# Pacing the bulk transfers of a fused attention and MLP kernel by the exponentials

## The chip, the cores and the metric

One core of a Trainium2 chip runs the whole kernel. The metric is the device time of one execution in microseconds, as the median of several runs. TensorE is written PE (and PEld for its weight loads), VectorE DVE, ScalarE ACT, GpSimd POOL, and SyncE SP; SP hands all transfers to the 16 DMA engines in one queue, in the order in which they stand on it.

## The reference

`x` has 2048 rows of 512 columns; there are 32 heads of 16 columns each, and the hidden layer has 1792 columns.

```python
x = A_x
xn = layernorm(x)                       # mean and variance over the 512 columns, eps 1e-5
qkv = xn @ wqkv                         # 512 x 1536, split into q, k, v of 32 heads x 16
p = softmax(q @ k.T * 16 ** -0.5)       # per head, 2048 x 2048
attn = (p @ v) @ wo
mlp = gelu_tanh(xn @ w1 + b1) @ w2 + b2
out = x + attn + mlp
```

## The kernel before

Precision is kept by pairs: an operand of a dense product is split into a high and a low float16 half, scaled by a power of two, and the product is three float16 products (`PAIRS`). The exponentials and `v` stay float32.

The attention runs over 32 blocks (8 groups of 4 heads, times 4 blocks of 512 queries), and each block over 16 units of 128 keys: 512 units, one after the other. In a unit, `s_half` computes scores for the maxima (`pS` on PE, a maximum on DVE), and `e_half` computes, for the unit that is 20 earlier (`LEAD`), transposed scores (`pT` on PE) and their exponential on ACT (`pe`, four of 128x512 a unit, L343). `v_half` multiplies the exponentials of one or two units before that by `v` (`pV`). Into each unit a planner lays a fixed share of the other dense work (`dense`, bank `pD`). In this text unit n is the one after which the counter `pos` stands at n; block t begins at unit 16t + 1 for the maxima, and at unit 16t + 21 for the exponentials.

In the first part (up to about unit 81) that other dense work is the projection of `q` and `k` for the heads of the later groups. A projection group has three units' worth of products (`project`); ACT copies its result to `pf`, POOL splits it into `stg`, and it is stored in DRAM (`qk_d`). `stacks` loads it from there as `kst` and `qst`, the operands of the scores, some 40 units before they are used. When the maxima of a block are known, DVE transposes them (`mrow`, L312), POOL splits them (`mhl`, L315 to L317), they are stored (`m_d`, L321) and loaded into two rows of each `qst` (L326); the exponentials of the block wait for these rows.

Beside that, the first part prepares the weights of the second (`prepare`): 16 chunks of 512 KB of `w1`, `w2` and `wo` are loaded (`wch`, three buffers), split on POOL in three steps (`split_steps`, to which the code gives costs of 1240, 1240 and 2330 ns; a `stg` pair has 620 and 1160), and the halves of `w1` and `w2` are stored (`wsp`, three buffers, to `w1_d` and `w2_d`, named `w_d` in the profile). Eight of the sixteen pieces of the normalised input are stored in this stage as well (`keep_x`, `xn_d`).

In the second part the other dense work is the MLP: `fetch_w1` loads `wc`, `fetch_x` a block of normalised input `xb` (one buffer, four pieces of 256 KB), and the `w2_s` pieces come one every three units. The third part is the output projection.

The order on every engine is that of the code, which is written unit by unit: `ORDERED` switches any reordering off. After each unit `tick()` runs what is due: `run_due()` calls what `later(n, fn)` has put n slots ahead, and `run_steps()` gives POOL queued steps worth up to `POOL_NS` = 2500 ns a slot. So a transfer stands on SP at the slot at which the code issued it, but SP carries it out as soon as the instructions before it on SP are handed over and what it waits for itself is done; it doesn't wait for the engines to reach that slot.

Of the kernel before, what the change touches and what calls it, by code (L numbers as in the profile page):

```python
# [11 lines left out]
AF = mybir.ActivationFunctionType  # L12
# [14 lines left out]
QB = 512  # L27
# [4 lines left out]
FAST, MEAN, SLOW, LATE = (8, 8), (7, 7), (6, 6), 6  # L32
MEASURE = (3, 0, 1, 2)
HALF = 1300
BEHIND = 4
POOL_NS = 2500
TAIL = 12
# [11 lines left out]
def layer_kernel(ctx: ExitStack, tc: tile.TileContext, x, wqkv, wo, w1, b1, w2, b2, out):  # L49
    nc = tc.nc  # L50
# [187 lines left out]
    def later(n, fn, local=False):  # L238
        queue.append((slot[0] + n, fn, local))

    urgent = []

    def run_due():
        while urgent:
            urgent.pop(0)()
        due = sorted((q for q in queue if q[0] <= slot[0]), key=lambda q: q[0])
        queue[:] = [q for q in queue if q[0] > slot[0]]
        for q in due:
            q[1]()
# [7 lines left out]
    def run_steps(all_of_them=False):  # L257
        room[0] = min(room[0], 0) + POOL_NS
        while steps and (room[0] > 0 or all_of_them):
            ns, fn = steps.pop(0)  # L260
            room[0] -= ns
            fn()

    def tick():
        run_due()
        run_steps()
        slot[0] += 1

    def flush():

        while steps or any(q[2] for q in queue):
            run_due()
            run_steps(True)
            slot[0] += 1

# [56 lines left out]
    def e_half(u, n):  # L332

        p, a = divmod(n, 2)
        t, kt = divmod(u, 16)
        g, qb = divmod(t, NQB)
        st = banks("T")
        r = slice(64 * a, 64 * a + 64)
        k0 = (kt % 4) * P
        tiled(None, st, kst[g % 2][p][kt // 4][r, k0:k0 + P], qst[g % 2][p][qb][r, :], True, True)  # L340
        pe = work.tile([P, QB], F32, name="pe", bufs=12)
        ptiles[u, n] = pe
        nc.scalar.activation(pe, st, AF.Exp, scale=factor(exp_scale, sexp[0:1, g // 2:g // 2 + 1]))  # L343
        given("act", 470)

    def v_half(u, a):
# [90 lines left out]
    def stacks(g, w, blocks):  # L437
        for b in blocks:
            for p in range(2):
                for a in range(2):  # L440
                    h = 4 * g + 2 * p + a
                    nc.sync.dma_start((qst, kst)[w][g % 2][p][b][64 * a:64 * a + 48, :],
                                      qk_d[w, h * DH:(h + 1) * DH, :, b * QB:(b + 1) * QB].rearrange("d j n -> (d j) n"))


# [151 lines left out]
    def fetch_x(b):  # L597
        if b < NQB:
            xbs[b] = feed[0].tile([P, 2, NC, QB], F16, name="xb", bufs=1)
            first = next(d for d in range(1, 17) if b == 0 or 2 <= (pos[0] + d) % 16 <= 11)  # L600
            for c in range(NC):
                later(first + c, lambda c=c: nc.sync.dma_start(xbs[b][:, :, c], xn_d[:, :, c, b * QB:(b + 1) * QB]))

    def fetch_w1(n):
        if n < NQB * NF:
# [107 lines left out]
    with ExitStack() as st1:  # L713
# [10 lines left out]
        def chunk(src):  # L724
            wf = ph.tile([P, 4 * W], F32, name="wch", bufs=3)
            v = wf.rearrange("p (a b) -> p a b", b=src.shape[2])
            if len(loads) < 17:
                nc.sync.dma_start(v, src)
            else:
                later(2, lambda: nc.sync.dma_start(v, src), True)  # L730
            return v

        def absmax(dst, v):
            nc.vector.tensor_reduce(dst, v, axis=AX.XY if len(v.shape) == 3 else AX.X, op=ALU.max,  # L734
# [24 lines left out]
        loads = []  # L759
# [83 lines left out]

        def keep_x(t):
            c, cols = t % NC, slice(t // NC * QB, t // NC * QB + QB)
            nc.sync.dma_start(xn_d[:, :, c, cols], xt[:, :, c, cols])

        def tile_and_unit(t):

# [122 lines left out]
        def prepare():  # L972
            yield from ms
            am = work.tile([P, 10], F32, name="am_all")
            nc.vector.tensor_reduce(am[:, 0:7], amx[:, 0:7, :], axis=AX.X, op=ALU.max)
            nc.vector.tensor_reduce(am[:, 7:8], b1_s, axis=AX.X, op=ALU.max, apply_absolute_value=True)
            nc.vector.tensor_reduce(am[:, 8:9], amx[:, 7:14, :], axis=AX.XY, op=ALU.max)
            nc.vector.tensor_reduce(am[:, 9:10], amx[:, 14:16, :], axis=AX.XY, op=ALU.max)
            box = []
            yield  # L980
            yield from scales(am, 10, sbank, box)
            inv, fac = box
            fac1.append(fac)

            nc.vector.reduce_max(gs[:, 0:1], fac[:, 0:8], axis=AX.X)
            nc.vector.tensor_tensor(gs[:, 3:4], fac_v[0][:, 0:1], fac[:, 9:10], op=ALU.mult)
            yield
            nc.vector.reciprocal(gs[:, 1:2], gs[:, 0:1])
            nc.vector.tensor_tensor(gs[:, 2:3], gs[:, 0:1], fac[:, 8:9], op=ALU.mult)
            yield  # L990
            nc.vector.tensor_scalar_mul(gs[:, 1:2], gs[:, 1:2], 0.5)
            ended = [True]
            for n in range(16):
                v = fetch(16 + n)
                while not ended[0]:
                    yield
                ended[0] = False

                def then(wh=None, n=n):
                    ended[0] = True  # L1000
                    later(2, lambda: put(wh, n), True)

                def put(wh, n):
                    for a in range(2):
                        if n < 7:
                            later(a, lambda a=a: nc.sync.dma_start(w1_d[n, :, a], wh[:, a]), True)
# [18 lines left out]
        ctx.enter_context(tc.manual_schedule(engines=ORDERED))  # L1025
        fil, pre, more = rest(), prepare(), True
        while not spent[0] or more or cur[0] is not None:
            unit(fil)
# [5 lines left out]
    def mlp():  # L1034
# [236 lines left out]
```

## Time and profile before

| | us |
|---|---|
| median of 3 runs (1473.83 to 1477.21) | 1473.98 |
| time of the profiled execution | 1471.34 |
| span of the profiled execution | 1469.5 |
| first exponential | 127 |
| end of the first part, about | 305 |

| queue or engine | |
|---|---|
| bytes moved by SP's transfers | 118.72 MB |
| their packets' time as a share of 16 DMA engines | 26.5% |
| PE, share of the span busy | 98% |
| POOL, share of the span busy | 50% |

A page row of an engine gives its busy time, its share of the span and its instruction count. A stage row gives start, end and length in us, and then for PE, PEld, DVE, ACT and POOL the busy time with the count in brackets, the clock granted to TensorE, the share of time that the DMA engines were busy and the GB/s they moved. A timeline row gives the start, the duration, the engine, the line, the operation, its output and inputs; behind it in square brackets stand the idle time of the engine before it and what ended it. "issue" there is time in which the engine waited for nothing that the profile shows. Chain and wait rows name lines of the code shown above.

### The profile page before, as it was taken

The page shows a single profiled execution, that of the slowest core. Times are in us where ns is not written, and L with a number is a line of the kernel's source. Part 1 is how long each engine was busy: PE and PEld are TensorE (multiplying, and loading weights), DVE is VectorE, ACT ScalarE, POOL GpSimd, SP SyncE. Part 2 cuts the span into 40 slices and gives each one's busy share as a digit, 9 for nine tenths or more (in the row PEclk, how much of TensorE's full clock was granted, in tenths as well). Part 3 has the DMA queues.
Part 4 walks back from the last instruction along what each step waited for, and adds up shares of the span by engine and source line. Part 5 has one row for each costly group of instructions (what it writes and reads, how often), then busy time and mean ns, then how long its engine had stood idle before and what let it go on. Part 6 is the DMA issues. An engine that isn't in the chain of part 4 may idle for free.

```text
span 1469.5 us, 87300 instructions
## 1 busy us (share of the span) xinstructions
PE 1445.6 (98%) x39753; PEld 928.6 (63%) x39753; DVE 1363.0 (93%) x2340; ACT 1230.0 (84%) x2326; POOL 737.5 (50%) x846
## 2 busy tenths in 40 slices
PE   8999989999999999999999999999999999999998
PEld 4434656666666666666666666666666666666674
DVE  7799998999999999999999999999999999999913
ACT  5325877899899999999998999999999999998884
POOL 4113598747766536556553655456475545551100
PEclk9999999999999999999999999999999999999999
DMA  6466457544111211121121211121101211102342
GB/s 205 154 185 176 137 183 241 171 127 117 59 42 44 88 51 37 45 58 53 38 66 45 63 44 45 30 75 50 56 26 54 78 37 35 29 24 73 112 130 102
DMA packets 118023, 124.30 MB, mean 85 GB/s; under 512 B 29080, under 2 KB 89624, under 8 KB 117652
## 3 DMA queue, kind: packets, MB, share of 16 engines
q1 hardware_dynamic: 117652, 118.72, 26.5%
q8 instruction: 310, 5.08, 1.4%
q14 instruction: 61, 0.50, 0.1%
HBM read 80.87 MB, written 37.60 MB: 81 GB/s over the span
## 4 chain that ended last, share of the span: by engine, by line
PE 90%; POOL 4%; DVE 3%; DMA 1%; issue 1%; ACT 1%; SPq 0%; DVEq 0%; POOLq 0%; ACTq 0%
PE pV L195 25%; PE pD L195 23%; PE pT L195 19%; PE pS L291 18%; PE pS L195 2%; PE pT L584 1%; DVE mt L292 1%; PE pV L584 1%; PE pS L485 1%; POOL wsp L969 1%; PE pT L485 1%; DVE amx L734 0%; PE pD L584 0%; PE pD L485 0%; POOL t L1053 0%
## 5 line engine op out<-in xcount | busy, mean ns | idle before, releaser
L292 DVE TENSOR_REDUCE mt<-pS 128x1 f32<-128x512 f32 x2048 | 1270.0, 682 | 35.5 <-PE pS L291 21.6
L343 ACT ACTIVATE pe<-pT 128x512 f32<-128x512 f32 x2048 | 1105.1, 599 | 133.8 <-PE pS L291 64.7
L195 PE MATMUL pV<-pe,vv 64*32 64x512 f32 x8192 | 1088.1, 599 | 0.5 <-issue 0.2
L195 PE MATMUL pT<-qst,kst 64*32 64x512 f16 x8192 | 658.8, 376 | 3.1 <-ACT pe L343 2.1
L291 PE MATMUL pS<-kst,qst 62*32 62x512 f16 x8192 | 621.6, 378 | 6.2 <-DVE mt L292 4.6
L195 PE MATMUL pD<-xb,wc 64*32 64x512 f16 x5376 | 372.0, 374 | 0.0
L195 PE MATMUL pD<-w_s,g 64*32 64x512 f16 (+1 forms) x6144 | 361.4, 348 | 0.6 <-POOL g L1054 0.4
L291 PEld LDWEIGHTS <-qst 62*32 62x32 f16 x8192 | 250.2, 92 | 136.6 <-issue 38.2
L195 PEld LDWEIGHTS <-kst 64*32 64x32 f16 x8192 | 250.3, 93 | 98.3 <-issue 12.7
L195 PEld LDWEIGHTS <-g 64*32 64x32 f16 x6144 | 197.4, 92 | 87.2 <-POOL g L1055 1.1
L195 PEld LDWEIGHTS <-wc 64*32 64x32 f16 x5376 | 178.3, 91 | 98.0
L195 PEld LDWEIGHTS pV<-pe,vv 64*32 64x32 f32 x8192 | 171.0, 105 | 6.6 <-PE pV L195 2.5
L1082 POOL TENSOR_SCALAR hh<-hh,fac,b_s 128x512 f32<-128x512 f32 x56 | 43.0, 768 | 223.9 <-ACT hh L1080 217.8
L195 PE MATMUL pD<-xt,wqk_h 64*32 64x512 f16 x1920 | 128.7, 375 | 2.3 <-issue 1.5
L1109 POOL TENSOR_TENSOR xa<-xa,yt 128x512 f32<-128x512 f32 x32 | 41.1, 1284 | 89.6 <-ACT yt L1107 89.6
L397 POOL TENSOR_TENSOR osb<-osb,rb 128x512 f32<-128x512 f32 x31 | 39.9, 1287 | 89.3 <-DMA rb<-den_d 86.7
L195 PEld LDWEIGHTS <-wqk_h 64*32 64x32 f16 x1920 | 60.8, 92 | 31.0 <-issue 5.9
L1053 POOL TENSOR_TENSOR t<-t,hh 128x512 f32<-128x512 f32 x56 | 71.8, 1282 | 4.7
L1060 POOL TENSOR_TENSOR t<-t,hh 128x512 f32<-128x512 f32 x56 | 71.8, 1281 | 4.7
L1055 POOL TENSOR_TENSOR g<-t,g 128x512 f16<-128x512 f32 x56 | 65.2, 1164 | 4.6
L1146 DVE SCALAR_TENSOR_TENSOR ac<-pS,gs,ac 128x512 f32<-128x512 f32 x20 | 14.4, 743 | 52.0 <-PE pS L195 40.3
L1058 POOL TENSOR_TENSOR t<-hh 128x512 f32<-128x512 f32 x56 | 58.2, 1040 | 4.1
(144 smaller groups left out, 908.1 us busy)
## 6 DMA issues: line engine op xcount, KB each, us to landing
wch<-in_B_w_dram SPq DMA_DIRECT2D x28, 512.0 KB
wc<-w_d SPq DMA_DIRECT2D x56, 256.0 KB
qk_d<-stg SPq DMA_DIRECT2D x32, 256.0 KB
rb<-den_d SPq DMA_DIRECT2D x31, 256.0 KB
w_d<-wsp SPq DMA_DIRECT2D x28, 256.0 KB
kst<-qk_d SPq DMA_DIRECT2D x128, 48.0 KB
qst<-qk_d SPq DMA_DIRECT2D x128, 48.0 KB
xs<-in_A_x_dram SPq DMA_DIRECT2D x16, 256.0 KB
```

Of the source, the lines that this page charges most:

```text
L195: p = nc.tensor.matmul(*args, **kw)
L291: nc.tensor.matmul(s[32 * j:32 * j + 32], qs[p][qb][r, c:c + 32], ks[p][kb][r, :], start=True, stop=True)
L292: nc.vector.reduce_max(mt_of[t][:, n, qt, kb:kb + 1], s, axis=AX.X)
L343: nc.scalar.activation(pe, st, AF.Exp, scale=factor(exp_scale, sexp[0:1, g // 2:g // 2 + 1]))
L397: pooled((1280, lambda: nc.gpsimd.tensor_tensor(osb, osb, rb, op=ALU.mult)), (620, lambda: nc.gpsimd.tensor_scalar(ot[:, 0], osb, 1.0, 0.0 ...
L485: nc.tensor.matmul(self.bank, lhs, rhs, start=start, stop=self.last and self.over())
L1053: (1280, lambda: nc.gpsimd.tensor_tensor(t1, t1, hh, op=ALU.mult)),
L1055: (1160, lambda: nc.gpsimd.tensor_tensor(g[:, 1, f, :], t1, g[:, 0, f, :], op=ALU.subtract)),
L1058: pooled((1040, lambda: nc.gpsimd.tensor_tensor(t1, hh, hh, op=ALU.mult)), (620, lambda: nc.gpsimd.tensor_scalar(t1, t1, 1.0, 1.0 / GELU_A ...
L1060: (1280, lambda: nc.gpsimd.tensor_tensor(t1, t1, hh, op=ALU.mult)),
L1082: later(1, lambda: pooled((690, lambda: nc.gpsimd.tensor_scalar(hh, hh, scale, bias, op0=ALU.mult, op1=ALU.add)), (0, lambda: gelu(hh, g, ...
L1109: add = lambda: nc.gpsimd.tensor_tensor(xa, xa, yt, op=ALU.add)
```

## The change

Two things are new. `paced` issues a transfer with an additional wait for the last exponential that has been handed to ACT up to this point of the program (`beat`). `batch` puts a transfer into a list instead of issuing it, and `run_bulk`, called in each slot between `run_due` and `run_steps`, issues from that list as long as a budget of 320 (KB, `BULK`) a slot is positive; each transfer counts 256, so it is one in most slots and two in every fourth.

Paced alone, at their old slots, are the stacks, the `xb` pieces and the `w2_s` pieces. Batched, and so paced too, are the weight chunks from the 18th load on (now in two halves of 256 KB), the stores to `w1_d` and `w2_d`, and the `xn_d` pieces of the first part. A chunk's split is now put to POOL's list only once both its halves have been issued (`landed`). Before the planned section starts (`timed`) nothing waits.

```diff
+BULK = 320
...
+    beat, timed = [None], [False]
+    def paced(*args):
+        p = nc.sync.dma_start(*args)
+        if timed[0] and beat[0]:
+            why = mybir.DependencyInfo(mybir.DependencyClass.Sync, mybir.DependencyReason.SCHED_ONLY)
+            tc.add_manual_dep(p.ins, beat[0], why, reason="pace")
+    bulk, budget = [], [0]
+    def batch(*args, then=lambda: None):
+        bulk.append((args, then))
+    def run_bulk():
+        budget[0] = min(budget[0], 0) + BULK
+        while bulk and budget[0] > 0:
+            args, then = bulk.pop(0)
+            paced(*args)
+            then()
+            budget[0] -= 256
...
     def tick():
         run_due()
+        run_bulk()
         run_steps()
...
-        nc.scalar.activation(pe, st, AF.Exp, scale=factor(exp_scale, sexp[0:1, g // 2:g // 2 + 1]))
+        p = nc.scalar.activation(pe, st, AF.Exp, scale=factor(exp_scale, sexp[0:1, g // 2:g // 2 + 1]))
+        beat[0] = p.ins.name
...
-                    nc.sync.dma_start((qst, kst)[w][g % 2][p][b][64 * a:64 * a + 48, :],
+                    paced((qst, kst)[w][g % 2][p][b][64 * a:64 * a + 48, :],
...
-                later(first + c, lambda c=c: nc.sync.dma_start(xbs[b][:, :, c], xn_d[:, :, c, b * QB:(b + 1) * QB]))
+                later(first + c, lambda c=c: paced(xbs[b][:, :, c], xn_d[:, :, c, b * QB:(b + 1) * QB]))
...
-                later(2, lambda: nc.sync.dma_start(v, src), True)
+                k, h = len(loads), src.shape[1] // 2
+                for a in range(2):
+                    batch(v[:, a * h:(a + 1) * h], src[:, a * h:(a + 1) * h], then=lambda a=a: a and landed.add(k))
...
-            nc.sync.dma_start(xn_d[:, :, c, cols], xt[:, :, c, cols])
+            (nc.sync.dma_start if t < 8 else batch)(xn_d[:, :, c, cols], xt[:, :, c, cols])
...
-                while not ended[0]:
+                while 16 + n not in landed or not ended[0]:
...
-                            later(a, lambda a=a: nc.sync.dma_start(w1_d[n, :, a], wh[:, a]), True)
+                            batch(w1_d[n, :, a], wh[:, a])
...
-                            later(a, lambda a=a: nc.sync.dma_start(w2_d[:, :, 2 * n - 14 + a], wh[:, :, a]), True)
+                            batch(w2_d[:, :, 2 * n - 14 + a], wh[:, :, a])
...
-            later(3 * k + 2, lambda k=k: nc.sync.dma_start(w2_s[:, :, k], w2_d[:, :, k]))
+            later(3 * k + 2, lambda k=k: paced(w2_s[:, :, k], w2_d[:, :, k]))
```

PE, DVE and ACT run the same instructions in the same order before and after; only SP and POOL differ. On SP, the transfers of units 33 to 36 stood like this (`L730` is the load of a chunk, `L1006` the store of a split one, `L846` a piece of `xn_d`; a name in brackets is a semaphore of a DMA or an engine):

```order
L846 DMA xn_d<-xt 256x1x512 [waits DMAHW7_49]
L730 DMA wch<-in_B_w_dram 128x4x256 [waits DMAHW0_49,DVE_49]
L730 DMA wch<-in_B_w_dram 128x4x256 [waits DMAHW1_49,DVE_49]
L1006 DMA w_d<-wsp 128x1024 [waits DMAHW2_49]
L730 DMA wch<-in_B_w_dram 128x4x256 [waits DMAHW3_49]
L548 DMA qk_d<-stg 128x2x512 [waits DMAHW4_49,Pool_49]
L549 DMA qk_d<-stg 128x512 [waits DMAHW5_49]
L1006 DMA w_d<-wsp 128x1024 [waits DMAHW6_49]
```

The first of these loads stood behind the `m_d` store and the `qst` rows of unit 33. In the changed kernel the first load stands ahead of them (`L247` is `paced`, and `Activation` the wait for the exponential):

```order
L247 DMA wch<-in_B_w_dram 128x2x256 [waits DMAHW6_49,DVE_49,Activation_49]
L247 DMA wch<-in_B_w_dram 128x2x256 [waits DMAHW7_49]
L345 DMA m_d<-mhl 128x2x32 [waits DMAHW0_49,Pool_49]
```

And in place of the rows shown of before there stand, in units 33 to 36:

```order
L247 DMA wch<-in_B_w_dram 128x2x256 [waits DMAHW1_49,DVE_49]
L247 DMA wch<-in_B_w_dram 128x2x256 [waits DMAHW2_49,Activation_49]
L247 DMA wch<-in_B_w_dram 128x2x256 [waits DMAHW3_49,Activation_49]
L573 DMA qk_d<-stg 128x2x512 [waits DMAHW4_49,Pool_49]
L574 DMA qk_d<-stg 128x512 [waits DMAHW5_49]
L148 DMA am_d<-am_qk 128x2 [waits DMAHW6_49,DVE_49]
L247 DMA wch<-in_B_w_dram 128x2x256 [waits DMAHW7_49,Activation_49]
L247 DMA xn_d<-xt 256x1x512 [waits DMAHW0_49]
```

The loads have become halves with a unit's exponential between them, and the stores of split chunks have moved behind them. On POOL, ahead of and behind the row of maxima of unit 49 (`mrow`, `mhl`), there stood:

```order
L967 TENSOR_SCALAR wch<-wch,inv_2411 128x2x4x128
L968 TENSOR_SCALAR wsp<-wch 128x2x512
L969 TENSOR_TENSOR wsp<-wch,wsp 128x2x512
L315 TENSOR_SCALAR mrow<-mrow 128x32
L316 TENSOR_SCALAR mhl<-mrow 128x32
L317 TENSOR_TENSOR mhl<-mrow,mhl 128x32
L563 TENSOR_SCALAR stg<-pf 128x512
L564 TENSOR_TENSOR stg<-pf,stg 128x512
```

And now:

```order
L588 TENSOR_SCALAR stg<-pf 128x512
L589 TENSOR_TENSOR stg<-pf,stg 128x512
L339 TENSOR_SCALAR mrow<-mrow 128x32
L340 TENSOR_SCALAR mhl<-mrow 128x32
L341 TENSOR_TENSOR mhl<-mrow,mhl 128x32
L996 TENSOR_SCALAR wch<-wch,inv_2411 128x2x4x128
L997 TENSOR_SCALAR wsp<-wch 128x2x512
L998 TENSOR_TENSOR wsp<-wch,wsp 128x2x512
```

The split of a chunk has moved behind the row of maxima, and a `stg` pair ahead of it. Over the whole first part the last split moves from unit 73 to unit 78.

More of the change, by code (lines that the diff above doesn't have):

```diff
@@ L269, in flush @@
     def flush():
-        while steps or any(q[2] for q in queue):
+        while steps or bulk or any(q[2] for q in queue):
             run_due()
+            run_bulk()
             run_steps(True)
@@ L729, in chunk @@
             else:
-                later(2, lambda: nc.sync.dma_start(v, src), True)
+                k, h = len(loads), src.shape[1] // 2
+                for a in range(2):
+                    batch(v[:, a * h:(a + 1) * h], src[:, a * h:(a + 1) * h], then=lambda a=a: a and landed.add(k))
             return v
+        landed = {16}
         def absmax(dst, v):
@@ L1025, in layer_kernel @@
         ctx.enter_context(tc.manual_schedule(engines=ORDERED))
+        timed[0] = True
         fil, pre, more = rest(), prepare(), True
```

## The prediction

> **What bounds the kernel now.** I read the page's busy shares first, then the busy time by stage, then the idle time of the stage that stands out.
>
> ```profile
> PE 1445.6 (98%) x39753; PEld 928.6 (63%) x39753; DVE 1363.0 (93%) x2340; ACT 1230.0 (84%) x2326; POOL 737.5 (50%) x846
> 200.00:240.00 40.00, 38.26 (x1124) 25.25 (x1114) 36.71 (x61) 31.97 (x60) 35.94 (x34) 1.00 0.60 195
> 440.00:480.00 40.00, 40.00 (x1204) 26.84 (x1196) 39.34 (x67) 36.98 (x72) 25.67 (x29) 1.00 0.14 41
> 176.70:268.30 91.60, 84.19 (x2416) 54.50 (x2401) 80.83 (x133) 71.53 (x135) 83.09 (x76) 1.00 0.67 208
> ```
>
> The columns of the last three rows are PE, PEld, DVE, ACT and POOL busy, then granted clock, share of the DMA engines and GB/s. TensorE sets the end: from about 400 us it has no gap (40.00 of 40.00). Only what makes TensorE stand still is worth time. Between 176.7 and 268.3 us it is idle for 91.60 - 84.19 = 7.4 us, at an undiminished clock; this is the stage in which the changed transfers run.
>
> How much that stage loses I read from ScalarE's evictions of the projection groups (`pf`), one a group of three units:
>
> ```profile
> 176.74 0.62 ACT L558 ACTIVATE pf<-pD 128x512 f32<-128x512 f32 x1
> 268.27 0.60 ACT L558 ACTIVATE pf<-pD 128x512 f32<-128x512 f32 x1
> 276.94 0.60 ACT L558 ACTIVATE pf<-pD 128x512 f32<-128x512 f32 x1
> 284.79 0.60 ACT L558 ACTIVATE pf<-pD 128x512 f32<-128x512 f32 x1
> 301.17 0.60 ACT L558 ACTIVATE pf<-pD 128x512 f32<-128x512 f32 x1 [0.25 <-PE pS L291]
> ```
>
> Ten groups lie between the first two rows: 91.53 / 10 = 9.15 us each. Three lie between the third and the last: 24.23 / 3 = 8.08 us, 2.7 us a unit. Ten at 8.08 would take 80.8 us, so the stage loses 10.7 us. The idle time in front of TensorE's weight loads shows where:
>
> ```profile
> 180.64 0.09 PEld L195 LDWEIGHTS <-wqk_h 64*32 64x32 f16 x2 [0.98 <-issue]
> 185.64 0.11 PEld L195 LDWEIGHTS <-wqk_h 64*32 64x32 f16 x7 [1.04 <-issue]
> 194.93 0.10 PEld L291 LDWEIGHTS <-qst 62*32 62x32 f16 x3 [1.74 <-issue]
> 199.57 0.09 PEld L291 LDWEIGHTS <-qst 62*32 62x32 f16 x3 [2.04 <-issue]
> 220.83 0.10 PEld L195 LDWEIGHTS <-kst 64*32 64x32 f16 x4 [1.49 <-DMA qst<-m_d]
> 249.01 0.09 PEld L291 LDWEIGHTS <-qst 62*32 62x32 f16 x2 [1.49 <-issue]
> 254.11 0.09 PEld L195 LDWEIGHTS <-wqk_h 64*32 64x32 f16 x2 [0.83 <-issue]
> 259.32 0.10 PEld L195 LDWEIGHTS <-wqk_h 64*32 64x32 f16 x3 [0.75 <-issue]
> PEld L291 <- issue: 7.1, 6, 2.0
> PEld L195 <- issue: 5.5, 8, 1.0
> PE pT L195 <- DMA qst<-m_d: 1.0, 1, 1.0
> ```
>
> The last three rows are the totals from 176 to 273 us (us, times, longest). All rows but two wait for "issue", that is for nothing the trace names: 7.1 + 5.5 = 12.6 us of the loads' time, part of it behind running matmuls. Neighbours are 4.6 to 5.2 us apart. The DMA part of the page has a queue of its own for instructions:
>
> ```profile
> q8 instruction: 310, 5.08, 1.4%
> 190.00:200.00 10.00, 7.16 (x207) 4.21 (x196) 8.80 (x15) 7.35 (x14) 9.59 (x8) 1.00 0.79 252
> 210.00:220.00 10.00, 9.86 (x300) 6.29 (x284) 9.97 (x18) 8.87 (x17) 9.50 (x11) 1.00 0.06 13
> 276.00:286.00 10.00, 10.00 (x304) 7.41 (x287) 9.84 (x16) 9.11 (x18) 8.23 (x7) 1.00 0.66 199
> GB/s 369 373 397 336 230 139 184 205 205 189 217 209 291 144 152 135 152 78 26 20 283 340 348 332 385 287 426 217 115 156 213 197 180 262 291 369 393 406 414 410
> ```
>
> 310 packets for 2 x 39753 TensorE instructions are 256 of them a packet. In 200:240 TensorE runs 1124 + 1114 instructions in 40 us, so 256 take 4.6 us: the spacing of the stalls. I read them as a packet of instructions that arrives late behind a long row of data. The last row gives 190 to 200 us in slices of 0.25 us: up to 426 GB/s, and at 410 when the worst stall ends. (276:286 has a share of 0.66 and no idle time: the share alone doesn't do it, the bunching does.)
>
> The Trainium skill (Runtime: NRT & Kernel Launch, "Instruction fetch mechanics") has blocks of 256 instructions, whose refill is "mostly hidden". The block size agrees with 256 a packet; the hiding does not hold here if my reading of the 4.6 us is right, and taken literally it would leave only the `qst<-m_d` stall to gain.
>
> **The change part by part.**
>
> *Pacing.* Before, SP hands over whatever its next instruction allows:
>
> ```profile
> 171.31 0.57 SPq L846 DMA_DIRECT2D xn_d<-xt  x1
> 171.99 1.40 SPq L730 DMA_DIRECT2D wch<-in_B_w_dram  x2
> 173.44 0.50 SPq L1006 DMA_DIRECT2D w_d<-wsp  x1
> 173.99 0.42 SPq L730 DMA_DIRECT2D wch<-in_B_w_dram  x1
> 174.51 1.15 SPq L548 DMA_DIRECT2D qk_d<-stg  x1
> 176.41 0.68 SPq L1006 DMA_DIRECT2D w_d<-wsp  x1
> ```
>
> These rows and the 128 KB store between the last two are 256 + 1024 + 256 + 512 + 256 + 128 + 256 KB = 2.7 MB in 5.8 us. At the 410 GB/s above that is 6.7 us of traffic, more than a block's 4.6 us. By the slots of the code, units 34 to 73 ask for up to 1.62 MB in a unit, 15 of them for over 1 MB. After the change the most there is 0.90 MB, or 2.2 us at 410 GB/s, inside a unit of 2.7 us and half of a block. So the row ahead of a block should rarely last long enough to stall it.
>
> The price is on SP alone. Each paced transfer stands behind the last exponential of its own unit, and behind it on SP stand the `m_d` store and `qst` rows of a later unit, the `qk_d` stores, the `den_d` steps and the `wc` loads, all of which need work of that unit or a later one anyway. A wait costs at most the part of one unit by which SP ran ahead. SP gets 15 more issues (half loads), at some 0.5 us each by the rows above: 7 us on an engine that mostly waits. I take 0 on the path; upper bound one unit, 2.7 us, at one place.
>
> *The second part* has no loss to remove (440:480). The transfer with the least room is the next block of `xb`:
>
> ```profile
> 510.86 3.15 SPq L602 DMA_DIRECT2D xb<-xn_d  x4
> 518.29 0.60 ACT L369 ACTIVATE osb<-pV 128x512 f32<-128x512 f32 x1
> 527.35 0.10 PEld L195 LDWEIGHTS <-wc 64*32 64x32 f16 x4
> ```
>
> Four pieces at once now, one a unit afterwards, the last with unit 165, whose own work ends near the `osb` row (518.3). With some 3 us to land it is there at 522, 5 us ahead of its first use at 527.35. Cost 0. The stacks are loaded two groups ahead, over 40 units; 0. The `w2_s` loads keep their slots; 0.
>
> *Load before split.* POOL's split of a weight chunk now enters the program only after its load was handed over, and POOL's order changes at three places. Before, POOL stood for a load that SP hadn't issued:
>
> ```profile
> 177.22 1.12 POOL L967 TENSOR_SCALAR wch<-wch,inv 128x1024 f32<-128x1024 f32 x1 [10.31 <-DMA wch<-in_B_w_dram]
> 210.63 0.20 DVE L312 STREAM_TRANSPOSE mrow<-mneg 128x32 f32<-128x32 f32 x1
> 215.43 0.23 POOL L315 TENSOR_SCALAR mrow<-mrow 128x32 f32<-128x32 f32 x1
> ```
>
> From 177.22 POOL runs without a real pause, so at 215.43 it takes up the row of maxima 4.6 us after VectorE gave it (210.83), and TensorE waits 1.49 us for the `qst` rows that follow (220.83). Without that wait 4.6 - 1.5 = 3.1 us of lag are free. In the new order this load stands one unit ahead of the row of unit 33 instead of behind it, so POOL should take it at 166.9 instead of 177.2, and one split (4.8 us by the costs that the code gives its POOL steps) moves behind the row of unit 49 while one `stg` pair (1.8 us) moves ahead of it. Following POOL's new list from there, with a load landing 3 us after its unit, I get a lag of about 2 us, under the 3.1. I take the stall as gone: -1.2 us on the path (between the 1.0 us of PE and the 1.49 us of its weight load). This part matters for the rest too: if POOL stayed late, what the blocks give back between 190 and 220 us would be lost at this stall.
>
> *Later end of the preparation.* The last split moves from unit 73 to 78. POOL has room there:
>
> ```profile
> 293.76 0.62 POOL L563 TENSOR_SCALAR stg<-pf 128x512 f16<-128x512 f32 x1 [6.43 <-ACT pf L558]
> 314.02 0.76 POOL L1082 TENSOR_SCALAR hh<-hh,fac,b_s 128x512 f32<-128x512 f32 x1 [6.03 <-DMA ot_d<-ot]
> ```
>
> 12.5 us of idle time against one split of 4.8 us behind unit 76; 0. But units 74 to 81 now carry 5.9 MB instead of 3.4, with 1.15 MB in units 76 and 79, or 2.8 us at 410 GB/s: one or two short stalls, +0.5 us.
>
> **Sum.**
>
> ```profile
> L175 ACT ACTIVATE wqk_h<-wq,inv 128x512 f16<-128x512 f32 x4 | 2.9, 726 | 0.0
> ```
>
> Of the 10.7 us lost, 1.2 are the `qst` stall and some 0.7 the two weight casts that ScalarE does in this stage and not in the next (half of their 1.45 us, by this row of 120 to 300 us, since ScalarE has room); 8.8 are late instruction blocks. Bounds: 0 of them removed, or all. I take 85%, since the row ahead of a block falls to half a block's time: -7.5. With -1.2 and +0.5: -8.2 us. From the profiled execution's 1471.3 us that is 1463; the median of the runs is 2.6 us higher, and 1474.0 - 8.2 gives 1465.8. About 0.3% (4.4 us) is what a measurement of this kernel can tell from no change.
>
> **The rivals.**
>
> *The blocks stay late.* If what delays a block is that data is in flight at all, not how much of it is queued, the smoothing leaves it: the volume is the same. Then the gain is the `qst` stall and perhaps a quarter of 8.8: -3, 1471. For it: the share in the stage must stay near 0.6. Against it: 276:286. The Trainium skill (DMA: Bandwidth & Descriptors, "Queues, rings and completion order") says that an engine takes turns between queues, packet by packet, so that the depth of one wouldn't hold up the other; this rival is that rule. No trace here shows the turns. Chance 0.18.
>
> *The bunching only moves.* The heavier units 74 to 81 stall at every block, four to five times 1 us: -8.2 + 4 = -4, 1470. Against it: 276:286, where 199 GB/s cost nothing. 0.12.
>
> *POOL becomes the bound (slower).* A chunk now passes through two paced loads before its split, and POOL, busy for 83.1 of 91.6 us here, has 9% to catch up with. If it lags at the rows of units 49, 65 and 81, TensorE pays each us over 3.1 three times. The gain is spent at a lag of 3.1 + 8.2 / 3 = 5.8 us; at 8 us (it once stood 10.31 for one load) the result is 3 x 4.9 - 8.2 = +6.5, 1480. For it: 9% is little. Against it: the code hands POOL at most 2.5 us of work a unit of 2.7. 0.07.
>
> *All of it and more.* If the groups come down to the 7.85 us of the shortest (276.94 to 284.79), the stage gains 13: 1461. 0.08.
>
> **How the numbers follow.** The forecast has the rest, 0.55. Faster by over 0.3% (below 1469.6): nearly all of 0.55, 0.08, half of 0.12 = 0.67. Within: the rest of these and 0.18 = 0.26. Slower: 0.07. The range 1460 to 1472.5 holds the forecast with its bounds (all 8.8 or half of them), the fuller gain and most of the two smaller ones; outside are the slower case and the tails.
>
> **What will show it.** Right: idle time of PEld put down to issue between 176 and 270 us falls from some 12 us to under 3; `pf` comes every 8.1 us; POOL takes the row of unit 49 within 3 us; `qst<-m_d` no longer stalls TensorE; GB/s in 0.25 us slices shows gaps between units. Wrong: the same stalls every 4.6 to 5.2 us at a smoother traffic; or `mrow` late on POOL three times; or new waits for `xb` in the second part.

## The result: 1% slower

| | before | after |
|---|---|---|
| median of the runs (6 each, same chip) | 1477.02 us | 1491.22 us |
| ratio, with 95% interval | | 1.0099 (1.0070 to 1.0128) |
| time of the profiled execution | 1471.34 us | 1485.74 us |

At 1477 us the ratio is a loss of 14.6 us; the forecast was a gain of 8.2. The chain of work that ended last, of the changed kernel and behind it of the kernel before:

```profile
PE 81%; DMA 5%; POOL 5%; DVE 3%; issue 2%; SPq 1%; ACT 1%; DVEq 0%; ACTq 0%; POOLq 0%
```

```profile
PE 90%; POOL 4%; DVE 3%; DMA 1%; issue 1%; ACT 1%; SPq 0%; DVEq 0%; POOLq 0%; ACTq 0%
```

TensorE has the same work (39753 products, 1447.6 us against 1445.6). On the chain, TensorE falls from 90 to 81%, and transfers rise from 1 to 5%: the end now waits for transfers. ScalarE's copy of a finished block of 16 units (`osb`) shows where. Three of the 32 ends of blocks, first of before, then of after:

```profile
272.13 0.60 ACT L369 ACTIVATE osb<-pV 128x512 f32<-128x512 f32 x1
314.73 0.64 ACT L369 ACTIVATE osb<-pV 128x512 f32<-128x512 f32 x1
355.47 0.64 ACT L369 ACTIVATE osb<-pV 128x512 f32<-128x512 f32 x1
```

```profile
272.44 0.60 ACT L394 ACTIVATE osb<-pV 128x512 f32<-128x512 f32 x1
321.36 0.62 ACT L394 ACTIVATE osb<-pV 128x512 f32<-128x512 f32 x1
366.08 0.62 ACT L394 ACTIVATE osb<-pV 128x512 f32<-128x512 f32 x1
```

Level until 272 us (+0.3), then +6.6 and +10.6; the last, at 1467 us, has +13.7. The step of 4.0 between the second and the third row lies in the second part, which should have cost nothing. The stage that the prediction looked at, of after (columns as there):

```profile
176.70:268.30 91.60, 82.70 (x2424) 52.36 (x2416) 78.87 (x134) 72.25 (x136) 63.48 (x59) 1.00 0.57 176
```

In 176.70 to 268.30 TensorE stood still for 8.9 us, where it had stood for 7.4, and POOL got through 63.5 us of work instead of 83.1. What was waited for from 176 to 273 us (us, times, longest):

```profile
PEld L196 <- issue: 8.7, 10, 2.7
PEld L315 <- issue: 0.8, 2, 0.6
PE pT L196 <- ACT pf L583: 4.5, 3, 2.2
PE pT L196 <- DMA qst<-m_d: 3.6, 2, 1.9
POOL wsp L997 <- issue: 13.6, 2, 8.7
POOL wsp L997 <- DMA w_d<-wsp: 9.0, 3, 5.3
```

The first row hides a success. Three of its ten pauses are TensorE's waits for `pf`; here are the three weight loads, the first with the `pf` that it waited for:

```profile
203.98 0.60 ACT L583 ACTIVATE pf<-pD 128x512 f32<-128x512 f32 x1 [1.85 <-POOL stg L589]
204.63 0.10 PEld L196 LDWEIGHTS <-kst 64*32 64x32 f16 x4 [1.54 <-issue]
215.03 0.10 PEld L196 LDWEIGHTS <-kst 64*32 64x32 f16 x4 [1.73 <-issue]
235.82 0.10 PEld L196 LDWEIGHTS <-kst 64*32 64x32 f16 x4 [2.74 <-issue]
```

`pf` itself waited for POOL's `stg`. Without these, 8.7 + 0.8 - 1.54 - 1.73 - 2.74 = 3.5 us are left of the 12.6 us of issue stalls before. These stalls went, as forecast, and new waits took the gain.

Not all of the 12.6 us were what the prediction took them for. "issue" in a row of a weight load says only that the load itself waited for nothing named; the product behind it can wait for something that is. At the two longest stalls of before, the rows of the products name VectorE's maxima:

```profile
194.92 0.40 PE L291 MATMUL pS<-kst,qst 62*32 62x512 f16 x4 [1.24 <-DVE mt L292]
199.57 0.40 PE L291 MATMUL pS<-kst,qst 62*32 62x512 f16 x4 [1.60 <-DVE mt L292]
```

Ahead of the first, VectorE had waited 1.12 us for a small transfer (`on`). A count of the weight loads tells the two kinds apart. With a product to each load, 128 loads are the 256 instructions of a packet. The stalls at 180.64, 230.26, 249.01, 254.11 and 259.32 have 2271, 3551, 4063, 4191 and 4318 loads ahead of them in the trace, so they are 1280, 512, 128 and 127 loads apart, multiples of 128 to within one; the two above have 2622 and 2702, 80 apart. From 176 to 270 us the loads' issue stalls at this place of a block (93 to 95 behind a multiple of 128) are 5.6 of 11.7 us before and 1.0 us after the change; TensorE's waits for VectorE's maxima are 3.2 us before and 0.2 after.

**The wait of the first part is a ring.** POOL stands 22.6 us for a free `wsp` buffer, that is for the store of an earlier split. The longest one, on POOL and SP, and SP's row of waits there (205 to 229 us):

```profile
216.75 0.24 POOL L341 TENSOR_TENSOR mhl<-mrow,mhl 128x32 f16<-128x32 f32 x1
217.02 0.37 SPq L345 DMA_DIRECT2D m_d<-mhl  x1
224.16 0.45 SPq L247 DMA_DIRECT2D w_d<-wsp  x1
226.84 1.04 POOL L997 TENSOR_SCALAR wsp<-wch 128x1024 f16<-128x1024 f32 x1 [8.74 <-issue]
```

```profile
SPq L345 <- POOL mhl L341: 9.1, 1, 9.1
```

SP stands 9.1 us at the `m_d` store until POOL, late itself, has made `mhl`. The next store of a split stands behind it and leaves at 224.16. POOL waits until 226.84; the row names no releaser, but by the semaphores in the trace it is this store. So POOL waits for SP, which waited for POOL; `stg` and `pf` are late next, and then TensorE.

SP's long wait itself is not new. In the kernel before it stood 10.0 us for `mhl` at this store (first row, 176 to 273 us, two waits with 13.3 us in all), and POOL went on without a wait:

```profile
SPq L321 <- POOL mhl L317: 13.3, 2, 10.0
219.31 1.04 POOL L968 TENSOR_SCALAR wsp<-wch 128x1024 f16<-128x1024 f32 x1
```

The next store of a split left SP only at 220.91 there, behind that row of POOL. What the change adds is that a store which POOL needs now stands behind the `m_d` store.

**The wait of the second part is SP's own time.** SP and POOL of after at the end of the block near 360 us, with TensorE's wait and SP's waits from 325 to 354 us; then the same place of before:

```profile
345.44 2.81 SPq L247 DMA_DIRECT2D qst<-qk_d  x4
349.33 0.25 POOL L341 TENSOR_TENSOR mhl<-mrow,mhl 128x32 f16<-128x32 f32 x1
351.83 1.41 SPq L247 DMA_DIRECT2D w_s<-w_d  x1
353.33 0.55 SPq L345 DMA_DIRECT2D m_d<-mhl  x1
357.56 2.62 SPq L350 DMA_DIRECT2D qst<-m_d  x4
360.28 0.40 PE L196 MATMUL pT<-qst,kst 64*32 64x512 f16 x4 [2.83 <-DMA qst<-m_d]
```

```profile
SPq L247 <- ACT pe L367: 3.1, 4, 2.1
```

```profile
342.87 0.25 POOL L317 TENSOR_TENSOR mhl<-mrow,mhl 128x32 f16<-128x32 f32 x1
343.27 0.54 SPq L321 DMA_DIRECT2D m_d<-mhl  x1
```

Here SP hands over stacks with hardly a pause in both kernels, and before it reached the `m_d` store 0.15 us behind `mhl` (343.27 against 342.87 + 0.25). With 3.1 us of waits for exponentials it reaches it 3.75 us behind (353.33 against 349.58). SP had no slack here, so what holds SP up comes out at TensorE. The waits are not the only thing that can do so at this end of a block; the table behind e8 takes them apart.

The loss is larger than the stall. Two stages of 2 us behind it, and four products of one kind ahead of and behind it:

```profile
360.00:362.00 2.00, 1.72 (x36) 0.77 (x44) 1.22 (x2) 1.08 (x2) 1.92 (x3) 0.68 0.14 40
362.00:364.00 2.00, 2.00 (x40) 0.95 (x32) 1.21 (x3) 0.90 (x2) 1.82 (x3) 0.50 0.68 233
```

```profile
356.83 0.61 PE L196 MATMUL pV<-pe,vv 64*32 64x512 f32 x4
361.55 1.08 PE L196 MATMUL pV<-pe,vv 64*32 64x512 f32 x4
```

The third column from the right is the granted clock: 0.50 behind the stall, and the same four products take 1.08 us instead of 0.61. From 360 to 364 us (0.68 and 0.50) that loses 0.64 + 1.00 = 1.6 us, beside the 2.8 us of standing still; some of it was made up again, the step of this block was 4.0.

### The profile page after: what moved, and what is told of

It is laid out like the page before. It is cut to its first block, busy times and chain, and to the rows that moved or that the text cites. A ratio compares the mean times of both kernels' runs of the same rounds, so it can differ in the third digit from the quotient of the medians.

```text
span 1484.0 us, 87421 instructions
## 1 busy us (share of the span) xinstructions
PE 1447.6 (98%) x39753; PEld 923.7 (62%) x39753; DVE 1361.1 (92%) x2340; ACT 1229.7 (83%) x2326; POOL 737.2 (50%) x846
## 4 chain that ended last, share of the span: by engine, by line
PE 81%; DMA 5%; POOL 5%; DVE 3%; issue 2%; SPq 1%; ACT 1%; DVEq 0%; ACTq 0%; POOLq 0%
PE pV L196 22%; PE pD L196 20%; PE pT L196 17%; PE pS L315 16%; PE pS L196 2%; DMA m_d<-mhl 2%; DVE mt L316 2%; DMA wch<-in_B_w_dram 1%; POOL wsp L998 1%; ACT pe L367 1%; DVE amx L763 1%; PE pT L609 1%; POOL stg L589 1%; DMA qst<-m_d 1%; PE pS L510 1%
```

## The experiments

Theories at the start: *stores* (the stores of splits come late and hold POOL), *SP* (the waits hold SP, and `m_d` and `qst` with it), and against them that the transfers themselves are slow, or that another part of the change smooths. The effect is the ratio less one, at the 1477 us of before beside it. The places are in this table: the `osb` row of each profiled execution minus that of before, in us; the column is the time in before.

| run | effect, us (95%) | 272 | 315 | 355 | 518 | 680 | 1165 | 1453 |
|---|---|---|---|---|---|---|---|---|
| the change | +14.6 (10.3 to 18.9) | 0.3 | 6.6 | 10.6 | 11.3 | 12.8 | 14.3 | 13.7 |
| e1, waits in first part only | +7.1 (4.9 to 9.3) | 0.5 | 4.9 | 6.2 | 6.9 | 6.9 | 7.8 | 9.6 |
| e2, no waits | +2.1 (0.0 to 4.3) | 1.1 | 5.8 | 7.7 | 7.9 | 8.9 | 9.1 | 10.7 |
| e3, stores at old slots | +4.4 (1.2 to 7.7) | -5.6 | -6.6 | -1.0 | 0.9 | 2.8 | 6.4 | 8.0 |
| e4, waits only | +10.9 (6.8 to 15.2) | 0.1 | 0.1 | 2.6 | 4.3 | 8.3 | 11.4 | 11.6 |
| e6, e1 and e3 | -8.6 (-10.5 to -6.6) | -3.3 | -3.8 | -3.8 | -3.2 | -2.0 | -1.7 | 0.3 |
| e8, e2 and e3 | -8.1 (-10.5 to -5.8) | -5.2 | -5.8 | -6.1 | -5.9 | -5.8 | -5.0 | -4.2 |
| e10, stores ahead in the line | +15.1 (12.6 to 17.4) | 0.9 | 7.8 | 12.6 | 13.6 | 16.2 | 22.4 | 23.7 |
| e5, 512 KB a unit | +4.9 (1.9 to 7.7) | -1.6 | -2.7 | -1.2 | -0.5 | 2.1 | 9.2 | 9.9 |
| e12, 512 KB, no waits | -5.3 (-7.4 to -3.4) | -2.2 | -2.5 | -3.0 | -2.9 | -2.7 | -1.9 | -0.7 |

The lags say where, the effects how much: the profiled execution of before (1471.3) was a quick one against its medians of 1476.8 to 1477.8 in these comparisons, and b1 and b2 below, which are the kernel before up to 345 us, lag at 315 by 3.5 and 3.3 us. Differences of some 3 us there mean nothing by themselves.

**e1: waits in the first part only.**

```diff
+    timed[0] = False
     def mlp():
```

> The changed kernel, but the waits for an exponential end with the first part: blocks of xb, w2_s and stacks of the second part are handed over freely again. Theory SP (a paced transfer holds SP, so the m_d store and the qst rows behind it come late at the ends of blocks): the four late ends of blocks from 360 us on lose their qst<-m_d stalls (3.5, 1.0, 1.9, 1.4 us) and the steps between osb rows there return to those of before; of the 14 us lost 7.4 come back: about 1484 us. Rival transfers (the m_d row waits in the DMA queues behind stacks, whoever hands them over): the stalls stay, 1491 us. Both leave the first part, up to the osb row near 321 us, as in the changed kernel.

Measured: 1481.54 us, ratio 1.0048 (1.0033 to 1.0063). 7.5 us came back, as theory SP had it; steps behind 355 us are down to between 0.1 and 1.8 us a column. One part of the expectation failed: TensorE's stall near 360 us shrank only from 2.83 to 1.68 us. That the sum came out at the 7.4 us expected is in part luck.

**e2: no wait at all.**

```diff
-        timed[0] = True
```

> The changed kernel without any wait for an exponential; the batches, their order and their 320 KB a unit in the code stay. Theory SP: the stalls at ends of blocks go (7.4 us). Theory stores (stores of split chunks come late because they stand behind chunk loads and xn_d in one line, so POOL waits for a free wsp buffer, and stg, pf and mrow come late): the code's line is the same, so POOL still waits some 20 us for wsp and the first part keeps its loss of 6 us: together about 1484 us. Rival (the wait, not the line, makes the stores late): POOL's waits for wsp go as well and the first part gains what was forecast, 1470 us. If the smoothness came from the wait alone, PEld's issue stalls between 176 and 270 us are back at some 10 us, and it lands near before, 1477 us.

Measured: 1480.09 us, ratio 1.0014 (1.0000 to 1.0029). POOL still stands for `wsp`, 23.3 us: the code's line makes the stores late, without any wait. The time is better than expected (its profiled execution was the slowest of ten), and still no gain. So the waits are most of the loss of the whole change, and the line eats the gain. The later stalls at ends of blocks are gone, but not the one near 360 us:

```profile
348.56 0.25 POOL L341 TENSOR_TENSOR mhl<-mrow,mhl 128x32 f16<-128x32 f32 x1
352.16 0.55 SPq L345 DMA_DIRECT2D m_d<-mhl  x1
358.96 0.40 PE L196 MATMUL pT<-qst,kst 64*32 64x512 f16 x4 [2.30 <-DMA qst<-m_d]
```

Without any wait for an exponential SP reaches the store 3.35 us behind `mhl` (352.16 against 348.81). It hands over transfers from 325 to 352 us with 0.9 us of waits in all: it comes late out of the first part (its `den_d` store at 324.69, 7.8 us behind before, where `mhl` is 5.7 us behind) and has no slack to catch up.

**e3: stores at their old slots.**

```diff
-                            batch(w1_d[n, :, a], wh[:, a])
+                            later(a, lambda a=a: nc.sync.dma_start(w1_d[n, :, a], wh[:, a]), True)
```

(and the same for `w2_d`).

> The changed kernel, but the stores of split chunks to w1_d and w2_d are handed over at their old slots, without wait and outside the batches; loads, xn_d and stacks stay as changed. Theory stores: POOL's waits for wsp fall from 27 us to under 5, ACT pf <- POOL stg from 10 us to under 3, the osb row near 272 us comes 5 us earlier and the one near 321 us some 6 us; the end about 1484 us. Rival (POOL waits for paced loads instead, wch): the idle time moves to wch and the time stays at 1491 us. Theory SP alone: the first part stays as it is, 1491 us.

Measured: 1480.59 us, ratio 1.0030 (1.0008 to 1.0052). POOL's waits for `wsp` from 160 to 310 us, and the stage; issue stalls of TensorE's loads from 176 to 270 us are 2.1 + 1.0 us:

```profile
POOL wsp L997 <- DMA w_d<-wsp: 2.9, 2, 2.3
```

```profile
176.70:268.30 91.60, 88.58 (x2648) 60.34 (x2639) 85.85 (x145) 78.88 (x149) 81.61 (x74) 1.00 0.72 224
```

The first part gains most of what was forecast (6.6 of 8.2 us by the `osb` row at 315): TensorE idle for 3.0 us in the stage instead of 7.4, at a higher share of the DMA engines (0.72) and more GB/s (224) than before. Then the second part loses it. At 348 us TensorE waits for `qst`, and the clock is low for 6.8 us from 346.7 us on:

```profile
347.70 0.61 PE L196 MATMUL pT<-qst,kst 64*32 64x512 f16 x4 [3.34 <-DMA qst<-m_d]
```

**e4: the waits alone.**

```diff
-                    batch(v[:, a * h:(a + 1) * h], src[:, a * h:(a + 1) * h], ...)
+                later(2, lambda: paced(v, src), True)
```

(whole chunks; stores and `xn_d` likewise `paced` at their old slots).

> Every transfer at its slot of before and whole (no batches, no halves), but each of those that the change paces waits for the last exponential handed over. If the wait itself is the loss (theory SP in the wide sense): qst<-m_d stalls at ends of blocks as in the changed kernel, 7 us, and 1484 us or more; if the line of batches is the loss (theory stores): POOL's waits for wsp are gone, the first part is no later than before, and only the 7.4 us behind 321 us stay. The issue stalls of PEld stay at some 10 us if the 320 KB a unit smooth the traffic, and fall to under 4 if the wait does.

Measured: 1483.75 us, ratio 1.0074 (1.0046 to 1.0103). The first part is neither early nor late, POOL's waits for `wsp` are 2.5 us, and the steps at ends of blocks are there (2.4, 1.8, 4.0, 3.1 us between the columns). The issue stalls stay, 6.3 + 5.9 us from 176 to 270, and 6.1 us of them at the place of a block (5.6 before): the wait doesn't smooth.

**e6 and e8: both losses undone.** e6 has the edits of e1 and e3, e8 those of e2 and e3.

> The two edits of the runs before, together: stores of split chunks at their old slots without wait, and no waits behind the first part; chunk loads, xn_d and the stacks of the first part stay batched or paced as changed. If the two losses are separate and add up, the first part keeps its gain of 6.6 us (osb near 308 us, where before has 314.73) and the second part loses nothing but about 1 us: near 1470 us against 1477, a ratio of 0.996. Rival (the later ends of blocks lose whatever was gained, because the gain only moves work against the transfers): the time stays near 1477 us or above.

> Only the line of chunk loads and xn_d with 320 KB a unit is kept: no wait for an exponential anywhere, stores of split chunks at their old slots. Theory line (the code's line smooths, the wait adds nothing): PEld's issue stalls between 176 and 270 us are at 3 to 4 us as in the run with waits, and the time is that of the run that undoes both, near 1470 us. Rival (the wait smooths): issue stalls near 10 us, and no gain, 1477 us.

Measured: e6 1470.45 us, ratio 0.9942 (0.9929 to 0.9955); e8 1469.09 us, 0.9945 (0.9929 to 0.9961), against 1477.79. Both are faster than the kernel before and after, and alike, so the wait adds nothing to the line. Issue stalls of PEld from 176 to 270 us are 3.6 + 2.6 = 6.2 us in e8, more than the "3 to 4" expected and half of before, and 6.1 us in e6, with the waits of the first part. At the place of a block they are 1.6 and 3.6 us.

The two losses don't simply add: undone alone they give 7.5 and 10.2 us back, together 23.2. How long SP's `m_d` store comes behind `mhl`, and how long TensorE then waits for `qst<-m_d`, at three ends of blocks (named by the columns above), shows why:

| run | SP behind, 355 | TensorE waits | SP behind, 518 | TensorE waits | SP behind, 680 | TensorE waits |
|---|---|---|---|---|---|---|
| before | 0.15 | 0 | 0.03 | 0 | 0.03 | 0 |
| the change | 3.75 | 2.83 | 1.67 | 0.52 | 1.63 | 1.20 |
| e1 | 3.02 | 1.68 | 0.03 | 0 | 0.03 | 0 |
| e2 | 3.35 | 2.30 | 0.43 | 0 | 0.40 | 0 |
| e3 | 3.35 | 3.34 | 2.25 | 1.30 | 1.80 | 1.51 |
| e4 | 3.38 | 2.77 | 1.94 | 1.37 | 2.97 | 2.36 |
| e6 and e8 | 0.03 | 0 | 0.03 | 0 | 0.03 | 0 |

At the first of these ends each fault is enough by itself: the waits with a first part that is on time (e4) or early (e3), and the late first part with no wait there (e1, e2). So undoing one of them leaves that stall in place. The later stalls come with the waits alone. The early first part of e3 paid more at 348 us (3.34 us, and 6.8 us of low clock) than the late one of the change at 360 (2.83 and 3.4).

**e10: stores ahead in the line.**

```diff
-        bulk.append((args, then))
+        k = sum(b[2] for b in bulk) if ahead else len(bulk)
+        bulk.insert(k, (args, then, ahead))
```

(with `ahead=True` for the stores alone).

> The changed kernel with all its waits, but stores of split chunks enter the line ahead of the loads and xn_d that stand in it. Theory stores in its strict form (the place in the line makes them late): POOL's waits for wsp fall from 27 us to under 5, and the osb row near 272 us comes as early as with stores at their old slots, 266 to 268 us; the second part keeps its stalls, 1481 us in all. Rival (the 320 KB a unit and the wait make them late, wherever they stand): waits for wsp stay over 10 us; or the loads behind them become late instead, POOL waits for wch, and the time stays at 1488 to 1491 us.

Measured: 1494.13 us, ratio 1.0102 (1.0085 to 1.0118). The strict form of theory stores falls. POOL no longer waits for `wsp`; it waits for loads (160 to 310 us; the second row names another transfer, but this step of a split reads only the load):

```profile
POOL wch L997 <- DMA wch<-in_B_w_dram: 16.5, 4, 9.7
POOL wch L997 <- DMA qst<-qk_d: 12.0, 2, 10.5
```

So whatever stands last in the line is late. By the code the line carries 15 chunks as 30 half loads, 28 stores and 8 `xn_d` pieces, 66 transfers of 256 KB; at 320 KB a unit that takes 52.8 units, in a first part that had 56 for it (units 17 to 73). With 94% of its slots taken in the mean, the line can't make up for a stretch in which more enters it than leaves.

**e5 and e12: a larger rate.** `BULK = 512`, with and without the waits.

> The changed kernel with 512 KB a unit instead of 320, that is two transfers of 256 KB a unit instead of five in four units; waits, order and contents of the line as changed. Theory rate (the line is too slow for what it carries: two half loads and two stores, 1 MB, for each chunk, so whatever stands last in it is late): POOL's waits for wsp and wch fall from over 25 us to under 8, the osb row near 314.73 comes some 5 us before that of before, and only the second part's stalls stay: near 1482 us. Rival (a store that waits for an exponential is late at any rate): waits for wsp stay over 10 us and the time at 1488 us or above. If 512 KB a unit no longer smooth, PEld's issue stalls from 176 to 270 us go from 4 us back to 10 us.

> The same, 512 KB a unit, without any wait for an exponential: everything of the change but the waits, at a larger rate. Theory rate: neither the stores nor the ends of blocks are late, 1470 us as with the stores outside the line. Rival (stores are late in any line): 1478 to 1480 us, as with 320 KB without wait.

Measured: e5 1481.35 us, ratio 1.0033 (1.0013 to 1.0052); e12 1472.35 us, 0.9964 (0.9950 to 0.9977), against 1477.73. POOL's waits for `wsp` and loads of e5 (160 to 310 us) that the trace puts down to a transfer fall to 3.0 + 1.5 us; 4.2 us more at these two steps it puts down to engines.

The rate was it, and the stores may stay in the line if it is fast enough. Issue stalls are 7.2 us in e5 and 8.1 us in e12 (before 11.7), but that does not show a faster line to smooth less: at the place of a block they are 1.8 and 1.2 us, no more than at 320 KB, and TensorE waits 2.3 and 4.3 us for VectorE's maxima, which in e12 was held by the small transfers `on` and `dn` (2.03 and 1.97 us). Whether e12 gains less than e8 is open, as the intervals overlap.

**b1 and b2: the disputed stall by itself.** The kernel before with 16 MB of added stores that nobody reads, over 64 units of the second part.

```diff
+    def extra(n):                                # b1, n counts units from 96 on
+        if n % 16 == 4:
+            for k in range(4):
+                nc.sync.dma_start(dd[n // 16 * 4 + k], vv[:, 4 * k:4 * k + 4, 0:512])
+    def extra(n):                                # b2
+        nc.sync.dma_start(dd[n // 4][:, n % 4], vv[:, n % 16, 0:512])
```

> The kernel before, with 16 MB of added stores from vv to a DRAM buffer that nobody reads, over 64 units of the second part (some 345 to 520 us): 4 MB at once in every sixteenth unit. Theory refill (TensorE's instructions arrive in packets of 256 and come late behind a long row of data): each 4 MB last some 10 us, with two to three packets in them; idle time of PEld put down to issue of 1 to 2 us at each, 8 to 20 us in all, 1485 to 1495 us. Rival (TensorE's idle time in the first part belongs to that part's work and not to the traffic): no new idle time, 1477 us.

> The same added 16 MB in the same 64 units, 256 KB in each unit. Theory refill: no row ahead of a packet is long, no new idle time, 1477 to 1479 us. Rival (any traffic delays the packets, by its volume): as much idle time as with 4 MB at once.

Measured: b1 1493.10 us (two executions), ratio 1.0109 (1.0073 to 1.0146); b2 1484.30 us, 1.0042 (1.0018 to 1.0066). At 1477 us that is 16.1 us (10.8 to 21.6) and 6.2 us (2.7 to 9.7). The stretch of the added stores, of before, and of b1 and b2, which need some 20 us longer for the same work:

```profile
345.00:520.00 175.00, 174.23 (x5124) 114.25 (x5120) 170.78 (x288) 159.73 (x307) 113.49 (x127) 1.00 0.22 65
```

```profile
345.00:540.00 195.00, 183.34 (x5236) 115.97 (x5225) 175.73 (x296) 164.63 (x314) 114.97 (x131) 0.98 0.45 148
```

```profile
345.00:540.00 195.00, 184.63 (x5272) 117.82 (x5267) 176.78 (x298) 165.15 (x315) 115.09 (x131) 0.98 0.47 148
```

At the same 148 GB/s TensorE is idle for 11.7 us with 4 MB at once and 10.4 us with 256 KB a unit, against 0.8 us before; but not in the same way. Each of the four bunches of b1 has its one long issue stall, of 2.7 to 3.2 us in front of a weight load (368.74, 415.60, 453.42 and 499.36). The first, and the stages between the four:

```profile
368.74 0.12 PEld L195 LDWEIGHTS <-wc 64*32 64x32 f16 x7 [3.16 <-issue]
368.74:415.60 46.86, 42.67 (x1152) 25.64 (x1152) 40.14 (x67) 38.10 (x72) 28.62 (x32) 0.96 0.51 171
415.60:453.42 37.82, 35.18 (x1025) 22.46 (x1025) 33.83 (x57) 32.00 (x61) 23.50 (x27) 1.00 0.40 139
453.42:499.36 45.94, 43.51 (x1280) 28.71 (x1280) 42.42 (x71) 39.84 (x76) 26.09 (x29) 1.00 0.40 134
```

Between them lie 1152, 1025 and 1280 weight loads: nine, eight (and one on the rim) and ten times 128. TensorE stands still at the borders of blocks of 256 of its instructions, the size of a packet of the instruction queue. So bunched traffic does delay these packets, in a part that had hardly any of these stalls and none of the first part's work. The trace gives no time at which a packet was asked for, so what in the transfers delays it stays open.

In b2, more than half of TensorE's idle time is one wait of another kind:

```profile
530.34 0.61 PE L195 MATMUL pT<-qst,kst 64*32 64x512 f16 x4 [5.93 <-DMA qst<-m_d]
```

SP, with the added stores to hand over, reached the `m_d` store 5.8 us behind `mhl` (522.15 against 516.36), and the store took another 5.1 us to land. This is the stall of the second part once more, and it is from b2's slowest execution of six; whether the others have it isn't shown. Issue stalls at the place of a block, from 345 to 540 us, are 17.0 us in b1, 8.9 in b2 and 1.0 before: spreading the same bytes halves them. It does not remove them, against the expectation.

## Why the prediction was wrong, point by point

- *What bounds the kernel* was right in its mechanism and wrong in its size. Blocks of 256 instructions do come late beside bunched transfers (b1), and the line takes these stalls away: at the place of a block 5.6 us before, and 0.3 to 3.6 us in every run with the line. But all of the 12.6 us of issue stalls were read as such blocks, and about half were; the two longest of the rows were waits for VectorE's maxima, which make 3.2 us of TensorE's 7.4 us of idle time there. These two lie 4.6 us apart, but not a block's 128 loads. In the change both kinds fell, to 3.5 us together (forecast: under 3), and three undisturbed groups, `pf` at 242.88 to 266.56, come every 7.9 us (forecast: 8.1). Kernels with the line but without its two faults gain 8.6 and 8.1 us, where the sum said 8.2; with the term mis-sized, that close an agreement is partly luck. The Trainium skill's "mostly hidden" refill (Runtime: NRT & Kernel Launch, "Instruction fetch mechanics"), which the prediction set against its reading, does not hold here: 3 us stood open at the border of a block at each bunch of b1. The rival that the blocks stay late falls, though b2's 8.9 us keep a part of it.
- *Pacing* failed, the step "I take 0 on the path". It listed what stands behind a paced transfer and called it harmless, since all of it needs later work anyway, and called SP "an engine that mostly waits". That is an average. At some ends of blocks in the second part SP works without pause, `mhl` was ready, and the `m_d` store waited for SP: 3.75, 1.67 and 1.63 us in the change, and 3.38, 1.94 and 2.97 us with the waits alone (e4). The bound, 2.7 us at one place, was exceeded at the first of them by the stall (2.83; 2.77 in e4) and more so with the clock behind it (4.0), and it came at several places: e1 puts the waits of the second part at 7.5 us.
- *The second part* failed with it ("the stacks are loaded two groups ahead, over 40 units; 0"). That asks whether the stacks are in time for their use, and they were. What was late stood behind them.
- *Load before split* and the rival *POOL becomes the bound* had the right place and the wrong transfer. I followed the loads in front of a split and left out the stores behind it, though they are in the same line and a split needs one of three `wsp` buffers. POOL took up the row of unit 49 8.6 us after VectorE gave it and that of unit 65 6.1 us after (at 216.15 and 263.16), above the 5.8 us from which the rival was to decide; a case that I gave 0.07. The `qst<-m_d` stall that was to go (-1.2) grew instead: TensorE waits 1.91 us at 221.29 and 1.73 us at 268.22. The check that was missing is one division: what the line carries, over its rate, against the units that it has: 52.8 of 56.
- *Later end of the preparation* was sized at +0.5. The lag to before grew by 6.3 us from 272 to 315. TensorE's waits in between are 2.0 us for `pf`, and so for `stg`, at 280.01, 0.9 us for `qst<-m_d` at 314.12, and 2.4 us at 320.56 for ScalarE's `hh`, which the trace puts down to a `qk_d` store. The first has the late splits ahead of it on POOL; for the other two the link to the line is likely, not shown.
- Missing altogether: the clock behind a stall.

## What to carry to other kernels

Before a wait is put on a queue that hands out work in order, read what that queue does in the busiest stretch, not its mean, and ask of every entry behind it whether it would otherwise have gone at once. A budget that smooths traffic must be set against what it has to carry: here a line 94% full made whatever stood last in it late, and at 59% (33 units of 56, at 512 KB) most of the gain was there. Smooth by the order of the program rather than by waits: the line alone gave the whole gain; taking the waits out gave 10 to 13 us (the change to e2, e3 to e8, e5 to e12), and they smoothed nothing (e4). And where a weight load waits for "issue", read the row of the product behind it, and count the instructions between stalls, before calling it late instructions.

## What the hardware showed beside that

A stall of 2 to 3.3 us can cost TensorE as much again: with TensorE standing still for 2.0 us in e1, 2.8 in the change and 3.3 in e3, the granted clock was 0.50 for 3.4, 3.4 and 6.8 us, which at half speed is 1.7, 1.7 and 3.4 us. In e1 and in the change it fell behind the stall, in e3 within it. It fell at two of b1's four stalls (368.74 and 499.36; 2.2 to 2.6 us of TensorE itself), and not behind four stalls of 1.9 to 2.4 us in the change (221.29, 235.81, 280.01, 320.56). The Trainium skill (TensorE: Matmul & The Clock Gate, "Part 1: The HAM clock gate") has the clock halved after an idle window of about 3.4 us that runs free of the kernel. The half agrees, and so do the 3.4 us and their double; here 2.0 us of standing still were enough.

The profiled execution of the change is the quickest of its six, with a mean granted clock of 0.996. The six have 0.991 to 0.998, 0.994 in the mean; the kernel before has means of 0.9955 to 0.9973 in the three comparisons of the experiments. At 1490 us the difference is 2 to 5 us of TensorE's time, an estimate from these clocks: that much of the 14.6 us can be the clock behind stalls.
